# Sums applied at the copy of the slot inputs, a product moved out of the middle of another, and expert weights doubled at pairs 3, 5, 7 and 9

## The chip, the cores and the metric

The kernel runs on one core of one Trainium2 chip. The metric is the device time of one execution in microseconds (us). The kernel before takes 405.17 us, the median of three runs (404.94 to 406.31). Everything is float32; products of TensorE read float32 or, in the last stage, pairs of rounded values (high part and rest).

## What is computed

Three layers in a row: causal attention in a window of 128 positions, a soft mixture of experts (8 experts with 4 slots each), and a feed-forward layer with a squared ReLU.

```python
scores = where((rel >= 0) & (rel < 128), q @ k.T / sqrt(64) - slope_h * abs(rel), -1e9)
attn = softmax(scores) @ v                    # 4 batches, 8 heads, 576 positions, 64
x = attn.transpose(0, 2, 1, 3).reshape(2304, 512)

logits = x @ phi                              # 2304 x 32
d = exp(logits - logits.max(0)); d /= d.sum(0) + 1e-9     # softmax over the tokens
slot_input = (d.T @ x).reshape(8, 4, 512)
slot_out[e] = relu(slot_input[e] @ w1[e]) @ w2[e]         # w1 512 x 1024, w2 1024 x 512
c = softmax(logits, axis=1)
y = c @ slot_out

out = relu(y @ w_in) ** 2 @ w_out             # 512 x 2048, 2048 x 512
```

## The kernel before

**Attention.** The work goes in 16 pairs of heads, u = 0 to 15 (4 batches with 4 pairs each), and in 72 steps of two chunks of 64 queries. One loop over the steps (L413) writes out the order of every engine's queue: the scores of the next step (emit_S), transposes, the products with v of a pair (emit_PV), then maxima, exponentials and sums. Work that belongs to a finished pair, such as the logits, is hung on a later step by the tables `side` and `side0` (L375 to L404) and issued by `run_side`.

**Loads.** All of them go through SP's queue. When a pair's last scores are issued, the loop loads query and key tiles of the pair after next (`load_q`, two tiles of 144 KiB and one of 288 KiB) and then one or two weight tiles of 1 MiB for later stages (`load_next_w`, L429). These fill a ring of 19 tiles; its 19 loads in attention are three of w1, seven more of w1 and nine of w2. At the end of attention, as buffers of attention come free, the rest of w1 follows: `load_extra` for six tiles or half tiles (w1 of the steps 3, 4, 5, 4, 6 and 7: 1, 0.5, 1, 0.5, 1 and 1 MiB), and `yw` (L493), which holds the weights of step 8. After that `pump` loads two pairs of f tiles (w_in and w_out) and the rest of w2 as ring tiles come free.

**The softmax over tokens.** It is kept as a running one: `nm` is the negative maximum so far for each row (4 groups of tokens by 32 slots), `zs` the sum, and `acc` the weighted sum of x, 128 rows by 512. For the last batch (b = 3) the steps stand written out after the loop, lines 466 to 539:

- logits of the remainder of pair 14 (L468), transposes of x (`emit_xn`), logits of pair 15, their copies into lgT and lgR, the new maximum, and `bm` (L479), the maxima spread over four columns by group;
- transposes of pair 15's x (X, L484; Y, L486), GpSimd's memset of siT (L494), transposes of all logits (W, L497), and the product `rep` by `bm` (G, L499) that gives each row the maxima of all four groups;
- the exponential dT (L501), `gm[0]` (L505), the factor between a group's maximum and that of all; the transposes of dT (L508, L509) and their copies into dn (L510, L511);
- R (L522, L524), dn by x in two halves of 256 columns, each added to acc (L529). Between the halves stands another product of `rep` (G, L528) that adds up the scaled sums of the four groups; from it come `gm[4]`, the reciprocal, and `ef` (L533), a matrix of 128 by 32 that adds up the groups, scaled with both factors;
- X (L537), acc by ef, four blocks of 128 rows, and the copy into siT (L539), where `diag` puts every slot into the columns of its own expert. All else in siT is zero.

**Experts.** `w1_step` (L608) takes siT by the w1 tile of a step into H, 16 steps with four products each; after the first eight the result is transposed and put through the ReLU (`emit_hT`), and 16 steps take it by w2 into O (L729). Then the combination weights, w_in and the slots' outputs are multiplied, and the last layer runs in units of 768 tokens by 128 features (emit_h, L768; emit_g, L811).

`keep_warm` issues products of the identity with itself whose result nobody reads.

Of the kernel before, what the change touches and what calls it, by code (L numbers as in the profile page):

```python
# [11 lines left out]
AF = mybir.ActivationFunctionType  # L12
# [16 lines left out]
def attn_moe_relu2_kernel(ctx: ExitStack, tc: tile.TileContext, z0, q, k, v, phi, w1, w2, w_in, w_out, bias, cst, out):  # L29
# [250 lines left out]
    def emit_logr(u):  # L280
        b, kk = divmod(u, NPAIR)
        for g in (b,) if b % 2 else (b, b + 1):
            pe.matmul(out=L_t[b][32 * g:32 * g + 32, 128:192], lhsT=phi_sb[:, kk, :], rhs=xT[u][:, rem(b)],
                      start=False, stop=(kk == 3), tile_position=(0, 32 * g), skip_group_check=True)
# [92 lines left out]
    for u in range(NU):  # L377
        t0 = (NCH * u + 8) // 2 + LT
        add = lambda dt, f, *a: side.setdefault(t0 + dt, []).append((f, a))
        side0.setdefault(t0 + 1, []).append((u,))  # L380
        add(1, emit_xT, u)
        late = u == NU - 1
        if late:
            break
        if u < NU - 2:
            add(4, emit_xn, u)
        if u % NPAIR == NPAIR - 1:
            for x in range(u - 3, u + 1):
                add(3, emit_logits, x)
            for x in range(u - 3, u + 1):  # L390
                add(3, emit_logr, x)
        if u == NU - 2:
            for x in range(u - 2, u + 1):
                add(3, emit_logits, x)
            for x in range(u - 2, u):
                add(3, emit_logr, x)
        if u % NPAIR == NPAIR - 1:
            b = u // NPAIR
            add(4, emit_d0, b)
            add(5, emit_d1, b)  # L400
            add(6, emit_de, b)
            add(8, emit_d2, b)
            add(9, emit_d3, b)
            add(9, emit_d4, b)  # L404
# [8 lines left out]
    for t in range(NS + LT + 1):  # L413
# [3 lines left out]
        if t + 1 < NS:  # L417
            emit_S(t + 1)
            if t in (0, 2):
                keep_warm("B", 1, idle)  # L420
            for u, c, n, e in info[2 * t + 2:2 * t + 4]:
                if c == NCH - 1:
                    if u + NQ < NU:
                        load_q(u + NQ)
                    if u == 0:
                        load_v(1)
                        sp.dma_start(out=tbl[:, 384:], in_=bias[:, 384:])
                        sp.dma_start(out=phi_sb, in_=phi)
                    for _ in range(0 if u == 0 else 2 if u > NU - 4 or u == 5 else 1):  # L429
                        load_next_w()  # L430
        if 0 < t - LT < NS:
            emit_T(t - LT)
# [32 lines left out]

    u, b = NU - 1, NB - 1
    p = slice(32 * b, 32 * b + 32)
    emit_logr(u - 1)  # L468
    emit_xn(u - 1)
    emit_logits(u)  # L470
    emit_logr(u)
# [19 lines left out]
    yw = six.tile([128, 4, 512], F32, name="yw")  # L491
    wt[wkey("w1", 8)] = yw
    sp.dma_start(out=yw, in_=w1[wkey("w1", 8)[1]].rearrange("p (a b) -> p a b", a=4))  # L493
    pool.memset(siT, 0.0)  # L494
    W = bank("B", "W")
    for bb in range(4):
        pe.transpose(W[:, 128 * bb:128 * bb + 128], lg(bb), ident)  # L497
    G = bank("S", "G")
    pe.matmul(out=G[:, 0:4], lhsT=rep, rhs=bm, start=True, stop=True)  # L499
    act.activation(out=xn_all[:, :, sl], in_=X.rearrange("p (g d) -> p g d", g=4), func=AF.Copy)  # L500
    act.activation(out=dT, in_=lg(b, 256), func=AF.Exp, bias=nm, scale=1.0, accum_out=stat[:, 4:5])  # L501
    act.activation(out=stat[:, 5:6], in_=stat[:, 3:4], func=AF.Exp, bias=nm, scale=-1.0)
    act.activation(out=xnr[:, sl], in_=Y[:, 0:128], func=AF.Copy)
    dve.tensor_reduce(out=gm[:, 1:2], in_=G[:, 0:4], axis=AX.X, op=ALU.min)
    act.activation(out=gm[:, 0:1], in_=nm, func=AF.Exp, bias=gm[:, 1:2], scale=-1.0)  # L505
    dve.scalar_tensor_tensor(out=zs, in0=zs, scalar=stat[:, 5:6], in1=stat[:, 4:5], op0=ALU.mult, op1=ALU.add)
    X = bank("T", "X")
    pe.transpose(X[:, 0:128], dT[:, 0:128], ident)  # L508
    pe.transpose(X[:, 128:256], dT[:, 128:256], ident)  # L509
    dve.tensor_copy(out=dn[:, 0:128], in_=X[:, 0:128])  # L510
    dve.tensor_copy(out=dn[:, 128:160], in_=X[:, 128 + 32 * b:160 + 32 * b])  # L511
    dve.tensor_tensor(out=gm[:, 2:3], in0=gm[:, 0:1], in1=zs, op=ALU.mult)
    act.activation(out=lgT.rearrange("p (h x) -> p h x", h=2)[:, :, 0:256], in_=W.rearrange("p (h x) -> p h x", h=2), func=AF.Copy)
    W = bank("xa", "W")
    pe.transpose(W[0:64, 0:128], lgR, ident)
    act.activation(out=lgNR, in_=W[0:64, 0:128], func=AF.Copy)
    keep_warm("S", 1)
    for hf in range(2):
        cl = slice(256 * hf, 256 * hf + 256)
        R = bank("T", "R")  # L520
        for g in range(4):
# [1 line left out]
                      tile_position=(0, 32 * g), skip_group_check=True)  # L523
        pe.matmul(out=R[p, 0:256], lhsT=dn[:, 128:160], rhs=xnr[:, cl], start=False, stop=True,  # L524
                  tile_position=(0, 32 * b), skip_group_check=True)
        if hf == 0:
            G = bank("S", "G")
            pe.matmul(out=G[:, 0:1], lhsT=rep, rhs=gm[:, 2:3], start=True, stop=True)  # L528
        dve.scalar_tensor_tensor(out=acc[:, cl], in0=acc[:, cl], scalar=stat[:, 5:6], in1=R[:, 0:256], op0=ALU.mult, op1=ALU.add)  # L529
        if hf == 0:  # L530
            dve.tensor_scalar(out=gm[:, 3:4], in0=G[:, 0:1], scalar1=1e-9, scalar2=None, op0=ALU.add)
            dve.reciprocal(out=gm[:, 4:5], in_=gm[:, 3:4])
            dve.tensor_scalar(out=ef, in0=e32, scalar1=gm[:, 0:1], scalar2=gm[:, 4:5], op0=ALU.mult, op1=ALU.mult)  # L533
    keep_warm("S", 1)
    X = bank("S", "X")
    for kk in range(4):
        pe.matmul(out=X[:, 32 * kk:32 * kk + 32], lhsT=acc[:, 128 * kk:128 * kk + 128], rhs=ef, start=True, stop=True)  # L537
    keep_warm("S", 2)
    dve.tensor_copy(out=diag(siT, 4), in_=X[:, 0:128].rearrange("p (a e s) -> p a e s", a=4, e=E))  # L539
    ps1.close()  # L540
    psum[0] = ctx.enter_context(tc.tile_pool(name="ps2", bufs=2, space=bass.MemoryType.PSUM))
    NBUF.update({"S": 2, "xa": 2, "T": 1, "U": 1, "xb": 1})
# [456 lines left out]
```

## Time and profile before

| | us |
|---|---|
| median of three runs | 405.17 (404.94 to 406.31) |
| the profiled execution | 405.26 |
| its span, first to last instruction | 403.3 |
| TensorE busy | 393.5 |
| VectorE busy | 291.7 |
| ScalarE busy | 245.3 |
| GpSimd busy | 90.4 |

Times in the profile count from the start of the span. Attention ends at about 130 us, the expert products start at 138.95 us and the last layer's products at about 175 us. An instruction's time in brackets is the idle time of its engine before it, with what ended it; "issue" means that the profile shows nothing it waited for. PE is TensorE's product, PEld its weight load, DVE VectorE, ACT ScalarE, POOL GpSimd, SP the engine that only issues DMAs. A float32 product takes two loads and two products; a transpose takes one of each.

### The profile page before, as it was taken

Reading aid. Unit: us, or ns where it says so; the run is one execution under the profiler, and the core shown is the slowest. Engines: PE = TensorE matmul, PEld = TensorE weight load, DVE = VectorE, ACT = ScalarE, POOL = GpSimd, SP = SyncE. Lnnn points to the kernel's source line nnn. Section 1 sums busy time; section 2 is a strip of 40 time slices with the busy share of each in tenths; the row PEclk is TensorE's granted clock in tenths of the full one; section 3 lists DMA queues with packets and bytes.
Section 4 is the critical chain, followed back from the end, with each engine's and each line's share of the span. In section 5 each row is a group of like instructions: output and inputs, shape, how many; then the busy total and the mean of one; then the engine's idle time right before and its main releaser. Section 6 shows DMA issues by size and latency. Waiting matters only on the chain.

```text
span 403.3 us, 7748 instructions
## 1 busy us (share of the span) xinstructions
PE 393.5 (98%) x2555; PEld 305.4 (76%) x2555; DVE 291.7 (72%) x957; ACT 245.3 (61%) x735; POOL 90.4 (22%) x188
## 2 busy tenths in 40 slices
PE   8999999999999999999999999999999999999995
PEld 7888878878876533378777888788877888888884
DVE  6798887879887685477778777697766874567455
ACT  5788878868876412177677765767657634443440
POOL 4545435334433041231211111112010000000000
PEclk9999999999999999999999999999999999999999
DMA  7879899768899999999305200000000040003004
GB/s 202 246 261 269 282 333 253 239 206 289 228 411 418 405 421 421 411 410 406 125 2 206 107 2 0 2 0 1 2 1 0 2 156 0 2 27 130 2 1 156
DMA packets 35944, 70.92 MB, mean 176 GB/s; under 512 B 20032, under 2 KB 21440, under 8 KB 31936
## 3 DMA queue, kind: packets, MB, share of 16 engines
q1 hardware_dynamic: 35328, 69.87, 48.1%
q10 hardware_dynamic: 576, 0.56, 0.4%
q8 instruction: 20, 0.33, 0.4%
q14 instruction: 20, 0.16, 0.1%
HBM read 65.70 MB, written 4.72 MB: 175 GB/s over the span
## 4 chain that ended last, share of the span: by engine, by line
PE 89%; DVE 6%; DMA 2%; ACT 1%; issue 1%; SPq 0%; POOL 0%; DVEq 0%; POOLq 0%; ACTq 0%
PE acc L811 49%; PE s L164 9%; PE xa L249 6%; PE h L768 4%; PE H L611 4%; PE O L729 3%; PE tp L215 2%; DVE ptb L239 2%; DMA kt<-in_k_dram 2%; PE X L290 1%; DVE p L172 1%; PE tq L217 1%; PE MX L697 1%; PE L L277 1%; DVE psum L829 1%; PE tq L223 1%
## 5 line engine op out<-in xcount | busy, mean ns | idle before, releaser
L811 PE MATMUL acc<-whl,arena_gh 128*128 128x512 f32 x864 | 218.2, 395 | 0.0
L811 PEld LDWEIGHTS acc<-whl,arena_gh 128*128 128x128 f32 x864 | 160.2, 188 | 37.1 <-issue 4.2
L797 DVE TENSOR_TENSOR arena_gh<-hT,arena_gh 128x384 fp32r<-128x384 f32 (+1 forms) x97 | 54.7, 564 | 33.3 <-ACT arena_gh L793 25.1
L196 POOL TENSOR_SCALAR p<-p,st 128x192 f32<-128x192 f32 (+1 forms) x142 | 56.2, 408 | 67.5 <-DVE ptb L239 28.1
L183 ACT ACTIVATE p<-p,st 128x192 f32<-128x192 f32 (+1 forms) x144 | 61.4, 429 | 11.6 <-DVE st L172 11.3
L780 ACT ACTIVATE acc<-h 128x384 f32<-128x384 f32 (+2 forms) x49 | 23.7, 484 | 67.3 <-PE h L768 67.2
L164 PE MATMUL s<-kt,zq 128*128 128x192 f32 (+2 forms) x288 | 58.3, 327 | 1.3 <-DMA kt<-in_k_dram 1.2
L657 POOL TENSOR_SCALAR yw<-f 128x512 f32<-128x512 f32 x32 | 26.0, 815 | 112.3 <-DVE arena_cin L674 59.8
L164 PEld LDWEIGHTS s<-kt,zq 128*128 128x128 f32 x288 | 44.8, 196 | 3.3 <-DVE ptb L239 0.9
L239 DVE COPY ptb<-tq 64x128 f32<-64x128 f32 x128 | 35.3, 281 | 14.8 <-PE tq L217 13.5
L172 DVE CUSTOM_DVE_ANT_0 p<-s,tbl 128x192 f32<-128x192 f32 (+1 forms) x144 | 41.7, 325 | 3.5 <-PE s L164 3.0
L237 ACT ACTIVATE ptb<-tp 128x256 f32<-128x256 f32 (+1 forms) x72 | 25.0, 348 | 13.1 <-PE tp L215 11.0
L768 PE MATMUL h<-cst_sb,Mst 128*128 128x384 f32 x96 | 31.9, 337 | 0.3 <-DVE Mst L708 0.3
L249 PE MATMUL xa<-ptb,vt 128*64 128x256 f32 (+1 forms) x256 | 27.8, 359 | 0.0
L183 ACT ACTIVATION_READ_ACCUMULATOR p<-p,st 128x1 f32 x144 | 27.3, 189 | 0.0
L789 DVE TENSOR_TENSOR hT<-acc 128x384 f32<-128x384 f32 (+1 forms) x18 | 9.7, 541 | 23.6 <-ACT acc L780 23.6
L215 PE MATMUL tp<-cs,p 128*128 128x128 f32 x128 | 26.5, 275 | 0.2 <-DVE st L187 0.2
L793 ACT ACTIVATE arena_gh<-acc 128x384 fp32r<-128x384 f32 (+2 forms) x49 | 25.0, 509 | 0.7
L793 ACT ACTIVATE arena_gh<-hT 128x384 fp32r<-128x384 f32 x48 | 24.8, 516 | 0.6
L249 PEld LDWEIGHTS xa<-ptb,vt 128*64 128x64 f32 x256 | 17.0, 136 | 9.4 <-issue 1.9
L672 DVE SCALAR_TENSOR_TENSOR yw<-f,yw 128x512 int32<-128x512 int32 x32 | 22.5, 707 | 1.0
L780 ACT ACTIVATE hT<-h 128x384 f32<-128x384 f32 x48 | 22.7, 472 | 0.0
(176 smaller groups left out, 455.4 us busy)
## 6 DMA issues: line engine op xcount, KB each, us to landing
w_w<-in_w_dram SPq DMA_DIRECT2D x30, 1024.0 KB, 8.2
f<-in_w_in_dram SPq DMA_DIRECT2D x16, 512.0 KB, 10.2
f<-in_w_out_dram SPq DMA_DIRECT2D x16, 512.0 KB, 10.2
vt<-in_v_dram SPq DMA_DIRECT2D x16, 320.0 KB, 7.3
zq<-in_q_dram SPq DMA_DIRECT2D x30, 144.0 KB, 4.3
kt<-in_k_dram SPq DMA_DIRECT2D x15, 288.0 KB, 4.4
out_dram<-psum SPq DMA_DIRECT2D x11, 256.0 KB, 2.1
w_w<-in_w_dram SPq DMA_DIRECT2D x2, 512.0 KB, 10.0
```

What stands on the lines that cost most here:

```text
L164: pe.matmul(out=sb_t[t][:, 256 * i:256 * i + n], lhsT=zq[u % NQ][:, c].rearrange("p a b -> p (a b)"), rhs=kt_t[u][:, 64 * c + 64 - n:64 * ...
L172: dve.tensor_tensor_reduce(out=p, in0=sb_t[t][:, 256 * i:256 * i + n], in1=tbl[:, 192 * pr + 192 - n:192 * pr + 192], scale=-0.125, scalar ...
L183: act.activation(out=p, in_=p, func=AF.Exp, bias=st[:, i:i + 1], scale=-1.0, accum_out=st[:, 2 + i:3 + i])
L196: eng.tensor_scalar(out=p, in0=p, scalar1=st[:, 4 + i:5 + i], scalar2=0.0, op0=ALU.mult, op1=ALU.add)
L215: pe.transpose(A[:, i, :], P[:, e:e + 128], ident)
L239: dve.tensor_copy(out=dst, in_=src)
L249: pe.matmul(out=out, lhsT=v_t[u][:, j, po:po + 64], rhs=pt[:, a:b, po:po + 64], start=(j == 0 or (j == 3 and a == 2)), stop=(j == 4 or (j ...
L768: pe.matmul(out=hb[-1][:, 0:HB], lhsT=Mst[:, 128 * f:128 * f + 128], rhs=cst_sb[:, c0:c0 + HB], start=True, stop=True)
L780: act.activation(out=rbuf[hf][:, cl], in_=hb[hf][:, cl], func=AF.Relu)
L793: act.activation(out=lo_t[i][1][hf][:, 0, cl], in_=rbuf[hf][:, cl], func=AF.Square)
L797: eng.tensor_tensor(out=gh[hf][:, 1, cl], in0=g[hf][:, cl], in1=gh[hf][:, 0, cl].bitcast(F32), op=ALU.subtract)
L811: pe.matmul(out=acc_t[s], lhsT=gh[:, x, c0:c0 + 128], rhs=w[:, f % 2, y, :], start=(f in firsts and a == 0), stop=(f in lasts and a == 2))
```

## The change

The scaling with the sums moves from `ef` to the copy into siT: `ef` is now e32 by gm[0] alone, `ez` is ef by zs, one product of a matrix of ones with ez (after both halves of R) gives the sum for each of the 32 slots in every row, and its reciprocal `zr` multiplies X on its way into siT. The product G of L528 between the halves is gone, and so are the two calls of keep_warm before R and after it. The first G (rep by bm) and what follows from it come after the transposes of dT and their copies. GpSimd fills `ones` (in phi_sb's place) at the point where it zeroed siT, and zeroes siT after dn is copied; a copy of one column of dn on GpSimd stands ahead of that. The logits of pair 14's remainder move from behind the loop into the table `side`. In the loop, two weight tiles are loaded at the pairs 3, 5, 7 and 9 instead of 5, 13, 14 and 15; the total stays 19.

```diff
--- before.py
+++ after.py
@@ -392,7 +392,7 @@
         if u == NU - 2:
             for x in range(u - 2, u + 1):
                 add(3, emit_logits, x)
-            for x in range(u - 2, u):
+            for x in range(u - 2, u + 1):
                 add(3, emit_logr, x)
         if u % NPAIR == NPAIR - 1:
             b = u // NPAIR
@@ -426,7 +426,7 @@
                         load_v(1)
                         sp.dma_start(out=tbl[:, 384:], in_=bias[:, 384:])
                         sp.dma_start(out=phi_sb, in_=phi)
-                    for _ in range(0 if u == 0 else 2 if u > NU - 4 or u == 5 else 1):
+                    for _ in range(0 if u == 0 else 2 if u in (3, 5, 7, 9) else 1):
                         load_next_w()
         if 0 < t - LT < NS:
             emit_T(t - LT)
@@ -465,7 +465,6 @@
 
     u, b = NU - 1, NB - 1
     p = slice(32 * b, 32 * b + 32)
-    emit_logr(u - 1)
     emit_xn(u - 1)
     emit_logits(u)
     emit_logr(u)
@@ -491,30 +490,34 @@
     yw = six.tile([128, 4, 512], F32, name="yw")
     wt[wkey("w1", 8)] = yw
     sp.dma_start(out=yw, in_=w1[wkey("w1", 8)[1]].rearrange("p (a b) -> p a b", a=4))
-    pool.memset(siT, 0.0)
+    ones = phi_sb.rearrange("p a b -> p (a b)")
+    pool.memset(ones, 1.0)
     W = bank("B", "W")
     for bb in range(4):
         pe.transpose(W[:, 128 * bb:128 * bb + 128], lg(bb), ident)
-    G = bank("S", "G")
-    pe.matmul(out=G[:, 0:4], lhsT=rep, rhs=bm, start=True, stop=True)
     act.activation(out=xn_all[:, :, sl], in_=X.rearrange("p (g d) -> p g d", g=4), func=AF.Copy)
     act.activation(out=dT, in_=lg(b, 256), func=AF.Exp, bias=nm, scale=1.0, accum_out=stat[:, 4:5])
     act.activation(out=stat[:, 5:6], in_=stat[:, 3:4], func=AF.Exp, bias=nm, scale=-1.0)
     act.activation(out=xnr[:, sl], in_=Y[:, 0:128], func=AF.Copy)
-    dve.tensor_reduce(out=gm[:, 1:2], in_=G[:, 0:4], axis=AX.X, op=ALU.min)
-    act.activation(out=gm[:, 0:1], in_=nm, func=AF.Exp, bias=gm[:, 1:2], scale=-1.0)
     dve.scalar_tensor_tensor(out=zs, in0=zs, scalar=stat[:, 5:6], in1=stat[:, 4:5], op0=ALU.mult, op1=ALU.add)
     X = bank("T", "X")
     pe.transpose(X[:, 0:128], dT[:, 0:128], ident)
     pe.transpose(X[:, 128:256], dT[:, 128:256], ident)
     dve.tensor_copy(out=dn[:, 0:128], in_=X[:, 0:128])
     dve.tensor_copy(out=dn[:, 128:160], in_=X[:, 128 + 32 * b:160 + 32 * b])
-    dve.tensor_tensor(out=gm[:, 2:3], in0=gm[:, 0:1], in1=zs, op=ALU.mult)
+    pool.tensor_copy(out=stat[:, 15:16], in_=dn[:, 159:160])
+    pool.memset(siT, 0.0)
+    G = bank("S", "G")
+    pe.matmul(out=G[:, 0:4], lhsT=rep, rhs=bm, start=True, stop=True)
     act.activation(out=lgT.rearrange("p (h x) -> p h x", h=2)[:, :, 0:256], in_=W.rearrange("p (h x) -> p h x", h=2), func=AF.Copy)
+    dve.tensor_reduce(out=gm[:, 1:2], in_=G[:, 0:4], axis=AX.X, op=ALU.min)
+    act.activation(out=gm[:, 0:1], in_=nm, func=AF.Exp, bias=gm[:, 1:2], scale=-1.0)
     W = bank("xa", "W")
     pe.transpose(W[0:64, 0:128], lgR, ident)
     act.activation(out=lgNR, in_=W[0:64, 0:128], func=AF.Copy)
-    keep_warm("S", 1)
+    ez, zr = dT[:, 128:160], dT[:, 160:192]
+    dve.tensor_scalar(out=ef, in0=e32, scalar1=gm[:, 0:1], scalar2=None, op0=ALU.mult)
+    dve.tensor_scalar(out=ez, in0=ef, scalar1=zs, scalar2=None, op0=ALU.mult)
     for hf in range(2):
         cl = slice(256 * hf, 256 * hf + 256)
         R = bank("T", "R")
@@ -523,20 +526,17 @@
                       tile_position=(0, 32 * g), skip_group_check=True)
         pe.matmul(out=R[p, 0:256], lhsT=dn[:, 128:160], rhs=xnr[:, cl], start=False, stop=True,
                   tile_position=(0, 32 * b), skip_group_check=True)
-        if hf == 0:
-            G = bank("S", "G")
-            pe.matmul(out=G[:, 0:1], lhsT=rep, rhs=gm[:, 2:3], start=True, stop=True)
         dve.scalar_tensor_tensor(out=acc[:, cl], in0=acc[:, cl], scalar=stat[:, 5:6], in1=R[:, 0:256], op0=ALU.mult, op1=ALU.add)
-        if hf == 0:
-            dve.tensor_scalar(out=gm[:, 3:4], in0=G[:, 0:1], scalar1=1e-9, scalar2=None, op0=ALU.add)
-            dve.reciprocal(out=gm[:, 4:5], in_=gm[:, 3:4])
-            dve.tensor_scalar(out=ef, in0=e32, scalar1=gm[:, 0:1], scalar2=gm[:, 4:5], op0=ALU.mult, op1=ALU.mult)
-    keep_warm("S", 1)
+    G = bank("S", "G")
+    pe.matmul(out=G[:, 0:32], lhsT=ones, rhs=ez, start=True, stop=True)
+    dve.tensor_scalar(out=zr, in0=G[:, 0:32], scalar1=1e-9, scalar2=None, op0=ALU.add)
+    dve.reciprocal(out=zr, in_=zr)
     X = bank("S", "X")
     for kk in range(4):
         pe.matmul(out=X[:, 32 * kk:32 * kk + 32], lhsT=acc[:, 128 * kk:128 * kk + 128], rhs=ef, start=True, stop=True)
     keep_warm("S", 2)
-    dve.tensor_copy(out=diag(siT, 4), in_=X[:, 0:128].rearrange("p (a e s) -> p a e s", a=4, e=E))
+    dve.tensor_tensor(out=diag(siT, 4), in0=X[:, 0:128].rearrange("p (a e s) -> p a e s", a=4, e=E),
+                      in1=zr.rearrange("p (e s) -> p e s", e=E).unsqueeze(1).to_broadcast([128, 4, E, SPE]), op=ALU.mult)
     ps1.close()
     psum[0] = ctx.enter_context(tc.tile_pool(name="ps2", bufs=2, space=bass.MemoryType.PSUM))
     NBUF.update({"S": 2, "xa": 2, "T": 1, "U": 1, "xb": 1})
```

## Rows read from the trace of the kernel before

**Rows 1.** The page: busy time by engine; shares of the chain that ended last
```profile
PE 393.5 (98%) x2555; PEld 305.4 (76%) x2555; DVE 291.7 (72%) x957; ACT 245.3 (61%) x735; POOL 90.4 (22%) x188
PE 89%; DVE 6%; DMA 2%; ACT 1%; issue 1%; SPq 0%; POOL 0%; DVEq 0%; POOLq 0%; ACTq 0%
```

**Rows 2.** Waits, 118 to 176 us: who waited, total us, times, longest
```profile
PEld H L611 <- issue: 7.4, 27, 0.3
```

**Rows 3.** Timeline of the hand-off: start, duration, engine, line, operation, idle before
```profile
...
134.74 0.16 PEld L522 LDWEIGHTS R<-xn_all,dn 128*32 128x32 f32 x8 [0.24 <-DVE dn L510]
...
135.74 0.30 PEld L528 LDWEIGHTS G<-stat,cs 128*128 128x128 f32 x2 [0.41 <-issue]
...
136.05 0.16 PEld L522 LDWEIGHTS R<-xn_all,dn 128*32 128x32 f32 x8
...
137.05 0.30 PEld L98 LDWEIGHTS warm<-cs 128*128 128x128 f32 x2 [0.41 <-issue]
...
137.16 0.48 DVE L529 SCALAR_TENSOR_TENSOR acc<-acc,stat,R 128x256 f32<-128x256 f32 x1 [0.23 <-PE R L524]
137.27 0.97 PEld L537 LDWEIGHTS X<-ef,acc 128*128 128x128 f32 x8
...
138.46 0.29 DVE L539 COPY siT<-X 128x128 f32<-128x128 f32 x1 [0.82 <-PE X L537]
...
138.95 0.19 PEld L611 LDWEIGHTS H<-w_w,siT 128*32 128x32 f32 x8 [0.27 <-issue]
...
138.98 0.29 DVE L559 TENSOR_TENSOR xnr<-lgT,acc 128x128 f32<-128x128 f32 x1
```

**Rows 4.** Timeline around the last pair: the remainder's logits and what follows
```profile
...
127.64 0.33 PEld L283 LDWEIGHTS L<-xT,phi_sb 128*32 128x32 f32 x4
...
130.44 0.14 PEld L283 LDWEIGHTS L<-xT,phi_sb 128*32 128x32 f32 x2
...
130.67 0.42 PEld L290 LDWEIGHTS X<-cs,xT 128*128 128x128 f32 x4
```

**Rows 5.** Timeline: GpSimd's memset of siT beside VectorE, and VectorE alone
```profile
...
132.66 0.95 POOL L494 MEMSET siT<- 128x1024 f32 x1 [5.69 <-PE Y L486]
...
133.12 0.51 DVE L479 TENSOR_SCALAR bm<-cs,stat 128x4 f32<-128x4 f32 x1
...
134.60 0.18 DVE L511 COPY dn<-X 128x32 f32<-128x32 f32 x1
```

**Rows 6.** Windows of 8 us: busy time by engine, granted clock, DMA share, GB/s
```profile
...
36.00:44.00 8.00, 8.00 (x108) 7.22 (x105) 6.78 (x37) 5.68 (x26) 3.75 (x10) 1.00 0.78 265
44.00:52.00 8.00, 7.73 (x65) 5.70 (x65) 6.87 (x41) 6.91 (x30) 3.96 (x10) 1.00 0.87 295
...
84.00:92.00 8.00, 8.00 (x70) 7.04 (x70) 6.35 (x34) 5.49 (x23) 2.76 (x8) 1.00 0.63 196
...
132.00:140.00 8.00, 7.41 (x64) 4.77 (x67) 4.89 (x21) 3.45 (x13) 0.95 (x1) 1.00 1.01 410
```

**Rows 7.** Key tile of the ninth pair: issue, landing time, first weight load
```profile
...
53.63 0.61 SPq L135 DMA_DIRECT2D kt<-in_k_dram  x1
...
DMA to landing us min/median/max: 5.2/5.2/5.2
...
59.42 0.53 PEld L164 LDWEIGHTS s<-kt,zq 128*128 128x128 f32 x4
```

**Rows 8.** Last expert weights: issues, landing time of yw, weight loads that waited
```profile
...
128.77 3.15 SPq L83 DMA_DIRECT2D w_w<-in_w_dram  x4
...
132.63 0.33 SPq L493 DMA_DIRECT2D yw<-in_w_dram  x1
...
DMA to landing us min/median/max: 13.3/13.3/13.3
...
145.98 0.16 PEld L611 LDWEIGHTS H<-yw,siT 128*32 128x32 f32 x8 [0.84 <-DMA yw<-in_w_dram]
...
168.47 0.31 PEld L729 LDWEIGHTS O<-w_w,hT 128*32 128x32 f32 x8 [0.55 <-DMA w_w<-in_w_dram]
```

## The prediction

> **What bounds the kernel now.** I read the page first: TensorE is busy for 98% of the span, and the chain that ended last lies on it for 89% [rows 1]. So only time in which TensorE waits, or an instruction that leaves its queue, can change the total. The waits of the stretch after attention come next. In the first product's weight loads 27 gaps of 0.27 us are put down to issue [rows 2]; they are the rhythm of four row groups, not a wait. Two loads stand out: the one on yw with 0.84 us and one in the second product with 0.55 us, both behind a DMA [rows 8]. Less their ordinary 0.27 to 0.30 us these are 0.56 and 0.25 us of real waiting. The timeline of the hand-off shows the rest: from 134.74 to 138.95 us one chain runs through R in two halves, acc, X, the copy into siT and the first expert load [rows 3]. The windows, last, say that the DMA engines are full there (share 1.01, 410 GB/s) and that TensorE's granted clock is 1.00, its upper level, 2.4 GHz [rows 6].
>
> **The change, part by part.** Times are in the profiled execution: 405.26 us, of which 403.3 us are span and 1.96 us lie around it. It is 0.09 us above the median of the runs, 405.17 us.
>
> *The sum of the exponentials leaves the middle of R.* Now the product G of line 528 stands between the two halves of R. From its load to that of the second half it takes 136.05 - 135.74 = 0.31 us [rows 3], and the second half, acc (L529), X and siT follow one on another. Taken out: -0.31 us. The new G (ones against ez) stands after the second half, where one keep-warm call stood. That call took 137.27 - 137.05 = 0.22 us up to X's first load [rows 3]; the new one has the same two loads as L528, so at most 0.31 us. X's later half waits for acc anyway, so between 0 and 0.09 us comes back; I take 0.09. The first, earlier G (rep against bm) moves from before the transposes of dT to behind them, into the gap of 0.24 us in which TensorE waits for dn [rows 3], where another keep-warm call is removed. The transposes may start up to 0.1 us sooner; they wait for the exponential too, so I take 0.
>
> *ScalarE and VectorE.* The exponential of gm now comes after the copy of lgT. Its readers are ef and ez, needed by the new G and by X, 2 us later. VectorE loses one small product; add and reciprocal grow from one column to 32, and ez is new. A copy of 128x32 out of PSUM takes 0.18 us [rows 5], so each is below some 0.2 us. Add and reciprocal run behind the second acc while TensorE works on X, which is ready 0.82 us after acc at the latest [rows 3]: two times 0.2 fit. If that cover were gone, they would cost up to 0.4 us. The copy into siT becomes a product of the same size; the copy took 0.29 us and a 128x128 product with a broadcast operand 0.29 us [rows 3]: 0.
>
> *GpSimd.* The memset of siT moves behind dn's copy, held there by a one-column copy. It takes 0.95 us [rows 5] and siT isn't written until 138.1 us, so GpSimd itself is in time. But VectorE's L479, four columns, took 0.51 us and ended at 133.63, 0.02 us after the memset, while a copy of 32 columns takes 0.18 us without one [rows 5]. The memset now lies where ef and ez are made. It can start when L511 ends, at 134.78, and a little later for the copy ahead of it; it ends at 135.8 to 136.1. If ef is held to its end, ef, ez and the first acc (0.48 us) follow, the last done at about 137.0, and the second acc, due at 137.16 - 0.31 = 136.85, starts up to 0.15 us late. Bounds 0 to 0.3 us; I take 0 in the sum and give the hold a case below. The Trainium skill, SBUF — State Buffer, section "SBUF: two separate sides", says that VectorE and GpSimd share one port pair under an exclusive lock and that the loser blocks for the other's whole instruction. The row of L479 agrees. By that rule ef is surely held, and the sum would be up to 0.15 us less of a gain, 404.2 to 404.35; without it the sum stands. The new memset of ones (128 columns of those 1024) needs the last reader of phi and has 4 us until its use: 0.
>
> *The remainder's logits of pair 14* leave the place after the last pair's products, where their two loads hold TensorE for 130.67 - 130.44 = 0.23 us, and join four like them that take 0.33 us, 0.08 us each [rows 4]. Two more there cost 0.16 us on the same queue, ahead of the last transposes and the last pair's products. Difference -0.07 us, with bounds 0 and -0.2; I take -0.05.
>
> *Weights.* Pairs 3, 7 and 9 load two tiles instead of 13, 14 and 15; pair 5 loads two before and after. Three tiles of 1 MiB leave the end of SP's queue; at 410 GB/s [rows 6] each takes 2.56 us. From 128.77 us on SP issues 1 + 0.5 + 1 + 1 MiB and then yw [rows 8]: 4.5 MiB or 11.5 us, which from an empty queue would be over at 140.3. yw landed at 132.63 + 13.3 = 145.9, so up to 5.6 us of older loads lay ahead. Three tiles fewer are 7.7 us fewer: the queue is empty at 128.77, and with 2 or 3 us of start (0 isn't seen in any row; the key tile with two tiles ahead took 5.2 [rows 7]) yw lands at about 142 to 143. It is wanted at 145.98 - 0.56 = 145.4, or 145.1 with the shorter hand-off. The wait is gone: -0.56 us. Behind yw lie two f tiles and seven of w2, 9 MiB or 23 us: 145.9 + 23 = 168.9, about where the load at 168.47 waited [rows 8]; then 165 to 166, wanted at 167.3. Gone too: -0.25 us.
>
> What is late next? Not a DMA; TensorE's own queue through both products. The f loads come 3 us sooner as well, but the stage after them waits on ScalarE: 0, with up to -0.4 in the range.
>
> *The price of the earlier tiles.* Each delays the query and key tiles of the pair after next. DMA idles for 0.22 x 8 + 0.13 x 8 = 2.8 us between 36 and 52 us, and for 0.37 x 8 = 3 us between 84 and 92 [rows 6]: room for 2.56. The narrowest cover I found is pair 8's key tile: landed 53.63 + 5.2 = 58.8, first used from 59.42, so 0.6 us [rows 7]. Price 0, bound +2.2 us (the third rival).
>
> **Sum.** -0.31 + 0.09 - 0.05 - 0.56 - 0.25 = -1.08 us, so 405.26 - 1.08 = 404.2 us.
>
> **Rivals.** First, the hold by the memset swallows what the hand-off gains: 405.26 - 0.56 - 0.25 - 0.05 + 0.1 = 404.5. For it: L479; against: ef isn't wanted before X, at 137.27 now [rows 3], and the later acc, not the first, sets the pace. Second, the tiles don't come sooner, since SP's queue is filled from elsewhere. Then yw lands at 145.9 as now, and whatever the hand-off gains is waited for again: 405.2. Against: in the code only the first two extra tiles, 1.5 MiB, are issued between the ring's last tile and 128.77. Third, slower: the tile of pair 3 is not taken up by the idle time. The key tile of pair 8 then lands at 58.8 + 2.56 = 61.4 instead of 59.42, TensorE stands for 1.9 us, and pair 9's for some 0.3 more: 404.2 + 2.2 = 406.4, beyond it if pair 7's does the same. It decides from 0.6 us of delay on; the 2.8 us idle speak against. Fourth, more gain: the earlier f loads also clear VectorE and GpSimd around the start of the last stage, and dT's transposes start sooner: 403.6. Fifth, the two removed keep-warm calls let the clock fall to 1.2 GHz. No stretch shows that level, through waits of 0.24 us and more, but if the 4.2 us from 134.74 to 138.95 ran at half the clock, it would be up to 4 us: 405.5 to 408.
>
> **How the numbers follow.** Forecast 404.2 (403.7 to 404.6): 0.57. Memset 404.5: 0.12. No sooner 405.2: 0.07. Late keys 406.4 and over: 0.09. More gain 403.6: 0.11. Clock: 0.04. What a measurement can tell here is about 0.3%, 1.2 us: faster is below 403.95, slower above 406.4. The fourth rival and the lower part of the forecast give 0.34 for faster; late keys and half of the clock 0.11 for slower; the rest is 0.55. The range leaves out most of the third and fifth rivals and the lowest edge: 403.4 to 405.4.
>
> **What would show it.** In the changed profile R's halves should follow each other with loads 1.0 us apart, the first expert load start some 0.3 us sooner after the last pair's products, and yw and the second product have no load behind a DMA. VectorE's ef beside the memset shows the first rival, a wait on the key tile around 43 to 60 us the third, a granted clock below 1.00 the fifth. The forecast is wrong if the first load of the last stage's products is less than 0.8 us sooner.

## The result, and the profile after

The changed kernel takes 407.81 us (median of 18 runs, 404.93 to 411.31) against 405.27 us for the kernel before, measured beside it (18 runs, 404.66 to 407.79): ratio 1.0053 [1.0034, 1.0072]. The ratio leaves out the longest of after's runs, which counts as a slow one; the medians of all runs lie 2.54 us apart. The loss is small but clear of the noise, and the time lies outside the range that was given. The profiled execution of after took 406.08 us, one of the quicker ones; its span is 404.0 us, 0.7 more than before's 403.3. So its trace shows the pattern of the loss, not the whole of it. Four of the 18 runs, at 409.2 to 410.4 us, had a mean granted clock of 0.995 to 0.996; none of these was profiled.

The page of after, busy time by engine and the chain that ended last by engine:

```profile
PE 392.7 (97%) x2551; PEld 304.2 (75%) x2551; DVE 292.4 (72%) x957; ACT 245.7 (61%) x735; POOL 90.6 (22%) x190
...
PE 85%; DMA 5%; DVE 5%; ACT 2%; issue 1%; SPq 1%; POOL 0%; DVEq 0%; POOLq 0%; ACTq 0%
```

Against [rows 1] the chain has moved from TensorE (89% to 85%) to DMA (2% to 5%). The waits of the attention stage, 8 to 126 us, say which DMA (who waited; total us, times, longest):

```profile
PE s L164 <- DMA kt<-in_k_dram: 2.2, 3, 0.9
...
PEld s L164 <- DMA kt<-in_k_dram: 0.8, 1, 0.8
```

The products wait 2.2 us on key tiles in three places (the load row is one of these waits once more, seen from the loads). Before had 1.2 us in the same stretch, all of it before 16 us, on the first keys:

```profile
PE s L164 <- DMA kt<-in_k_dram: 1.2, 2, 0.7
```

Which ones they are in after, TensorE's products say (start, duration, engine, line, operation, idle before and its releaser):

```profile
9.88 1.01 PE L164 MATMUL s<-kt,zq 128*128 128x64 f32 x6 [0.93 <-DMA kt<-in_k_dram]
...
44.02 0.68 PE L164 MATMUL s<-kt,zq 128*128 128x64 f32 x4 [0.69 <-DMA kt<-in_k_dram]
...
60.63 0.71 PE L164 MATMUL s<-kt,zq 128*128 128x64 f32 x4 [0.61 <-DMA kt<-in_k_dram]
```

The first belongs to the start; the others are the keys of pairs 6 and 8. The time from one pair's first product of L249 to the next shows what each cost: set beside before's, after is 0.45 us ahead up to pair 3 (35.27 against 35.72), 0.33 behind from 44.97 on, 1.19 from 61.59 on and 1.48 from 78.18 on. So late keys cost 0.78 + 0.86 + 0.29 = 1.93 us here. (The last 0.29 us is put down to the keys of pair 10, which landed at 77.1 us with their first product at 77.24; the profile names no wait there.)

The span falls into three parts at two such products, the second pair's (22.18 us in before, 21.73 in after) and the last pair's (128.54 and 130.14), here before's two and then after's:

```profile
22.18 1.74 PE L249 MATMUL xa<-ptb,vt 128*64 128x256 f32 x16
...
128.54 1.73 PE L249 MATMUL xa<-ptb,vt 128*64 128x256 f32 x16
...
21.73 1.73 PE L249 MATMUL xa<-ptb,vt 128*64 128x256 f32 x16
...
130.14 1.73 PE L249 MATMUL xa<-ptb,vt 128*64 128x256 f32 x16
```

| | start to second pair | to last pair | to the end | span |
|---|---|---|---|---|
| before | 22.18 | 106.36 | 274.76 | 403.3 |
| after | 21.73 | 108.41 | 273.86 | 404.0 |
| difference | -0.45 | +2.05 | -0.90 | +0.7 |

The first part is the start, which varies from one execution to the next and has nothing of the change in it. The stage that was to become shorter did, and the stage that pays for it lost more: the +2.05 are the 1.93 us of late keys and 0.11 of two loads that the change moves ahead of the last pair.

The windows of after, columns as in [rows 6] (the last two are DMA share and GB/s):

```profile
36.00:44.00 8.00, 7.33 (x100) 6.47 (x97) 6.75 (x39) 5.92 (x26) 3.30 (x9) 1.00 1.09 305
44.00:52.00 8.00, 7.71 (x65) 5.83 (x66) 6.17 (x38) 6.59 (x28) 3.74 (x10) 1.00 1.07 309
52.00:60.00 8.00, 7.67 (x66) 6.48 (x64) 6.42 (x34) 6.07 (x25) 3.37 (x9) 1.00 1.07 293
60.00:68.00 8.00, 7.36 (x63) 6.26 (x62) 6.13 (x40) 6.29 (x26) 3.31 (x9) 1.00 1.07 314
68.00:76.00 8.00, 7.73 (x95) 6.50 (x94) 5.91 (x34) 5.18 (x24) 3.81 (x10) 1.00 1.09 297
76.00:84.00 8.00, 7.75 (x64) 6.16 (x65) 6.60 (x40) 7.35 (x33) 3.14 (x8) 1.00 1.00 299
84.00:92.00 8.00, 8.00 (x67) 5.95 (x63) 6.03 (x32) 5.00 (x20) 2.74 (x7) 1.00 0.85 283
```

The share went from 0.78 and 0.87 [rows 6] to 1.09 and 1.07, but the rate only from 265 and 295 to 305 and 309 GB/s. Full of weight tiles alone the same engines move 410 [rows 6]. In the mix of attention they are full at about 300. (The share adds up the times of packets and can pass 1.)

Pair 8's key tile, the one the prediction named as the narrowest, in after: its issue at 54.0 us, and the time from issue to landing.

```profile
L135 SPq DMA_DIRECT2D kt<-in_k_dram x1: 613/613/613, 54.0 to 54.0; - x1
...
DMA to landing us min/median/max: 6.6/6.6/6.6
```

6.6 us instead of 5.2, so it lands at 60.6, where its first load began at 59.42 in before [rows 7]; this is the wait at 60.63 above. The two key tiles before it and the two behind it took 6.4 to 8.2 us (in before 3.9 to 5.6).

The hand-off in after, timeline:

```profile
129.13 0.44 PEld L283 LDWEIGHTS L<-xT,phi_sb 128*32 128x32 f32 x6
...
130.14 1.49 PEld L249 LDWEIGHTS xa<-ptb,vt 128*64 128x64 f32 x16 [0.17 <-issue]
...
132.04 0.42 PEld L290 LDWEIGHTS X<-cs,xT 128*128 128x128 f32 x4
...
136.03 0.37 PEld L525 LDWEIGHTS R<-xn_all,dn 128*32 128x32 f32 x11 [0.32 <-DVE dn L506]
...
136.25 0.95 POOL L509 MEMSET siT<- 128x1024 f32 x1
...
136.50 0.74 DVE L519 TENSOR_SCALAR ef<-cs,stat 128x32 f32<-128x32 f32 x1 [0.36 <-ACT stat L514]
...
137.28 0.24 DVE L520 TENSOR_SCALAR dT<-ef,stat 128x32 f32<-128x32 f32 x1
...
138.11 0.97 PEld L536 LDWEIGHTS X<-ef,acc 128*128 128x128 f32 x8
...
139.29 0.29 DVE L538 TENSOR_TENSOR siT<-X,dT 128x128 f32<-128x128 f32 x1 [0.32 <-PE X L536]
...
139.80 0.19 PEld L611 LDWEIGHTS H<-w_w,siT 128*32 128x32 f32 x8 [0.27 <-issue]
```

And the two loads that waited in [rows 8]:

```profile
146.26 0.16 PEld L611 LDWEIGHTS H<-yw,siT 128*32 128x32 f32 x4 [0.27 <-issue]
...
169.23 0.26 PEld L729 LDWEIGHTS O<-w_w,hT 128*32 128x32 f32 x8 [0.60 <-DMA w_w<-in_w_dram]
```

From the last pair's first product to the first expert load it is 9.66 us instead of 10.41. yw no longer keeps a load waiting; the tile of the second product still does. The windows of this stretch, columns as above, show the granted clock at 1.00 throughout:

```profile
128.00:136.00 8.00, 7.11 (x88) 5.23 (x87) 4.21 (x17) 4.39 (x14) 0.65 (x2) 1.00 0.76 256
136.00:144.00 8.00, 7.86 (x74) 4.09 (x78) 6.74 (x28) 1.38 (x5) 1.07 (x2) 1.00 1.01 413
```

### The profile page after: what moved, and what is told of

Its sections match the earlier page's. It is cut to its first block, busy times and chain, and to the rows that moved or that the text cites. A ratio compares the mean times of both kernels' runs of the same rounds, so it can differ in the third digit from the quotient of the medians.

```text
span 404.0 us, 7740 instructions
## 1 busy us (share of the span) xinstructions
PE 392.7 (97%) x2551; PEld 304.2 (75%) x2551; DVE 292.4 (72%) x957; ACT 245.7 (61%) x735; POOL 90.6 (22%) x190
## 4 chain that ended last, share of the span: by engine, by line
PE 85%; DMA 5%; DVE 5%; ACT 2%; issue 1%; SPq 1%; POOL 0%; DVEq 0%; POOLq 0%; ACTq 0%
PE acc L811 49%; PE s L164 7%; PE xa L249 5%; DMA kt<-in_k_dram 5%; PE h L768 4%; PE H L611 4%; PE O L729 3%; PE tp L215 2%; DVE ptb L239 2%; DVE p L172 1%; PE X L290 1%; PE MX L697 1%; PE tq L217 1%; DVE psum L829 1%; PE MY L703 1%
## 5 line engine op out<-in xcount | busy, mean ns | idle before, releaser
L164 PEld LDWEIGHTS s<-kt,zq 128*128 128x128 f32 x288 | 43.9, 193 | 5.6 <-issue 2.7
L249 PE MATMUL xa<-ptb,vt 128*64 128x256 f32 (+1 forms) x256 | 27.8, 359 | 0.0
L249 PEld LDWEIGHTS xa<-ptb,vt 128*64 128x64 f32 x256 | 17.0, 136 | 9.5 <-issue 2.0
```

The source lines that it names most:

```text
L164: pe.matmul(out=sb_t[t][:, 256 * i:256 * i + n], lhsT=zq[u % NQ][:, c].rearrange("p a b -> p (a b)"), rhs=kt_t[u][:, 64 * c + 64 - n:64 * ...
L249: pe.matmul(out=out, lhsT=v_t[u][:, j, po:po + 64], rhs=pt[:, a:b, po:po + 64], start=(j == 0 or (j == 3 and a == 2)), stop=(j == 4 or (j ...
```

## Experiments

The theory (A): the weight tiles at pairs 3, 7 and 9 fill the DMA queue of the attention stage, key tiles land late, and TensorE stands; the new hand-off is sound. The rival: the hand-off itself costs the time (the memset's hold, the clock without the keep-warm calls), and the late keys of one profile are chance. Every kernel was timed beside the kernel before, whose median was 405.73 us beside the first four kernels below, 405.4 beside the next four and 405.56 beside the last four. Each kernel has one profiled execution, and what is read from it can differ in another.

**The new hand-off alone**, with the old places for the doubled tiles:

```diff
-                    for _ in range(0 if u == 0 else 2 if u in (3, 5, 7, 9) else 1):
+                    for _ in range(0 if u == 0 else 2 if u > NU - 4 or u == 5 else 1):
```

> The changed hand-off with the weight loads of before (two tiles at pairs 5, 13, 14 and 15). Theory A (the time is lost in attention, where the earlier weight tiles make query and key tiles late): the hand-off is some 0.6 us shorter, but yw lands where it did, near 145.9 us, so the wait for it grows from 0.56 to about 1.2 us and the time stays at 405.2, within 0.4. Theory B (the new order of the hand-off itself costs, by GpSimd's memset beside VectorE): 407 to 408.

Measured: 405.26 us, ratio 0.9993 [0.9976, 1.0009]. The loss is gone, as theory A had it, so the hand-off isn't its cause. No gain can be measured either. Its profiled execution (407.63 us, its longest) shows one reason, the products' side of the first expert product:

```profile
148.08 1.07 PE L611 MATMUL H<-yw,siT 128*32 128x512 f32 x8 [1.45 <-DMA yw<-in_w_dram]
```

With the old schedule yw comes late for the shorter hand-off (in this execution it also landed some 0.9 us later after the last pair's first product than in before), and TensorE stands for it: from the last pair to the end it takes 275.71 us there, 0.95 more than before, though the hand-off in it is 0.75 shorter. From the second pair to the last it is 106.48 us, after's loss of 2 us gone.

**The new places alone**, in the kernel before (the places-only kernel from here on):

```diff
-                    for _ in range(0 if u == 0 else 2 if u > NU - 4 or u == 5 else 1):
+                    for _ in range(0 if u == 0 else 2 if u in (3, 5, 7, 9) else 1):
```

> The kernel before with two weight tiles at pairs 3, 5, 7 and 9, hand-off untouched. Theory A: key tiles of pairs 6, 8 and 10 land after they are wanted, 2 to 3 us of TensorE waiting in attention, less the 0.56 us of yw: 407 to 408.5. Theory B: nothing lost in attention, 404.5 to 405.

Measured: 407.88 us, ratio 1.0053 [1.0028, 1.0077], the whole of the loss. Its profiled execution was its longest (411.01 us), and shows what long runs of after may look like. Waits, 8 to 126 us:

```profile
PE s L164 <- DMA kt<-in_k_dram: 5.1, 5, 2.2
...
PEld s L164 <- DMA kt<-in_k_dram: 1.2, 1, 1.2
```

The load row again repeats one of the products'. The longest, 2.2 us, lies at 17.64 us, ahead of the first double; it is the start's, which put this execution 2.59 us behind before's. From the second pair to the last it takes 109.44 us, 3.08 more than before (1.18, 1.19 and 0.71 at pairs 6, 8 and 10), and from there to the end 274.99 (before 274.76). The granted clock stays at 1.00 in all windows from 36 to 92 us: these 3 us are waiting and not a lower clock. The loss that theory A expected is there.

**The same total at other pairs**: doubles at 5, 8, 9 and 13, with the new hand-off. Against before, two doubles have moved, to 8 and 9, where after has three, at 3, 7 and 9. (The diff is the same line with another set; so it is below with one extra tile and with two.)

> The changed kernel with two weight tiles at pairs 5, 8, 9 and 13, the same total of 19. In the trace of before the DMA engines are nearly idle from 74 to 78 and from 83 to 87 us, right behind the loads of pairs 8 and 9. Theory A: these places take the tiles without delay to a key tile, the hand-off's 0.6 us and most of the wait on yw are gained: 404.0 to 404.4. Theory B, or if any tile that is loaded earlier costs: 407 and over.

Measured: 405.30 us, 0.9989 [0.997, 1.0007]. From the second pair to the last it takes 106.48 us. Key tiles land in 4.4 us at the median between 30 and 100 us, as before's in 4.5 (after's: 6.5). The two doubles at 8 and 9 cost nothing here; the gain of some 1 us that was expected isn't there either.

**A cheaper query tile**: after, with {3, 5, 7, 9} kept, but each pair's query tile loaded whole, its zero halves included, in one transfer of 128 rows instead of two of 64 rows. (Part of the edit: the filling of the tiles with zeros on GpSimd at the start goes too, and the host lays q out with its zeros.)

```diff
-        z = zq[u % NQ]
-        sp.dma_start(out=z[0:64, :, 0, :], in_=q[u, 0:64].rearrange("p (c t) -> p c t", t=64))
-        sp.dma_start(out=z[64:128, :, 1, :], in_=q[u, 64:128].rearrange("p (c t) -> p c t", t=64))
+        sp.dma_start(out=zq[u % NQ].rearrange("p c a b -> p (c a b)"), in_=q[u])
```

> The changed kernel, but each pair's query tile is loaded as one transfer of 128 rows of 4608 bytes, zeros among them, in place of two of 576 pieces of 256 bytes: twice the bytes, no small packets. Theory A1 (large packets take longer while other DMA engines still move small ones, so the slowest of the 16 engines falls behind): key tiles land some 2 us sooner and the time falls to 404 to 405. Theory A2 (only the bytes count): 0.3 MB more in each pair, key tiles later still, 409 and over.

Measured: 405.27 us, 0.9992 [0.9979, 1.0004]. Twice the bytes for the queries, and the loss is gone with the schedule untouched. Windows of this kernel:

```profile
36.00:44.00 8.00, 8.00 (x107) 6.99 (x106) 6.72 (x36) 5.72 (x27) 3.97 (x10) 1.00 1.01 408
...
60.00:68.00 8.00, 7.46 (x65) 6.40 (x65) 6.92 (x41) 6.55 (x28) 4.08 (x11) 1.00 1.00 377
```

With the engines full (share 1.01, in after 1.09) the queue now moves 408 instead of 305 GB/s, key tiles land in 5.2 us at the median, 6.4 at most, and from the second pair to the last it is 106.48 us again. The time is a little above A1's range, and A2 is out. So the mix was slow because of the query transfers, not because of its bytes.

**One extra tile at a time** beside pairs 5, 13 and 14 (pair 15's double given up): pair 3, pair 7, pair 9.

> The changed kernel with two weight tiles at pairs 3, 5, 13 and 14: of the three that the change moves only one, to pair 3. The same with the loads of before took 405.26 us. Theory A with pair 3 as the cause (its tile is still in the queue when the tiles of pairs 6 and 8 are wanted): 406.3 to 407.3, key tile of pair 6 landing over 6 us after its issue. Rival (no tile costs alone, only three together overfill the queue): 405.0 to 405.6.

> The changed kernel with two weight tiles at pairs 5, 7, 13 and 14: only one moved, to pair 7. Theory A: pair 10's key tile lands later by about one tile's 2.5 us, of which 3.5 us were spare, so 405.3 to 406.0, less than pair 3's. Rival (only three together): 405.0 to 405.6.

> The changed kernel with two weight tiles at pairs 5, 9, 13 and 14: only one moved, to pair 9, behind which the DMA engines are idle for 3 us. Theory A: 404.9 to 405.4, no key tile late. Rival (any tile moved to before pair 13 costs): 406 and over.

Measured: 405.64 us, 1.0013 [0.9987, 1.0039]; 405.05, 0.9996 [0.9976, 1.0017]; 405.31, 0.9996 [0.9977, 1.0016]. None costs anything that can be told in the median. From the second pair to the last the profiles give 107.32, 106.50 and 106.50 us: only the double at pair 3 shows, with 0.9 us. Most of it, 0.7 us, comes where the keys of pair 8 are late, behind the double at pair 5 that stays:

```profile
59.98 0.71 PE L164 MATMUL s<-kt,zq 128*128 128x64 f32 x4 [0.44 <-DMA kt<-in_k_dram]
```

So no double here was quite alone.

**Two halves, whole rows**: as the cheap query tile above, but in two transfers of 64 rows, each with its zeros, so that count and rows are those of after and the length of a row is that of the cheap one.

(Part of the edit, against after; the rest is that of the one transfer.)

```diff
+        z = zq[u % NQ].rearrange("p c a b -> p (c a b)")
+        sp.dma_start(out=z[0:64], in_=q[u, 0:64])
+        sp.dma_start(out=z[64:128], in_=q[u, 64:128])
```

> As the one with whole query tiles of 128 rows of 4608 bytes (405.27 us), but again two transfers for each pair, of 64 rows each, as the kernel before issues them. If the small packets were what made key tiles late: 405.0 to 405.8, as with one transfer. If it was the third transfer on SP's queue and the 0.6 us by which the key tile is issued later: 406.5 to 408.

Measured: 423.8 us, 1.0435 [1.0389, 1.0482]; neither expectation holds. The page's row of these transfers (count, KB each, median us from issue to landing):

```profile
zq<-in_q_dram SPq DMA_DIRECT2D x30, 288.0 KB, 7.9
```

The trace notes when each of the 16 DMA engines is through with a tile, and tiles land in the order of their issue. With the same bytes as in the one-transfer kernel, in the same long rows, the second half of pair 6's query tile, 288 KB, landed 1.20 us behind the first (43.33 and 44.53 us, the first engine to land each); in the one-transfer kernel the whole 576 KB landed 1.47 us behind the tile ahead (39.01 and 40.48). By these distances, which are an estimate since neighbours overlap, a transfer that covers 64 rows runs at about 245 GB/s against 400. After's 144 KB halves land 0.8 us apart (41.77, 42.58, 43.36, the last engine), 180 GB/s. These have pieces of 256 bytes as well as 64 rows; the kernel with whole rows shows that the 64 rows are enough for a loss, and what the short pieces add isn't separated.

The Trainium skill, SBUF — State Buffer, sections "Door 1: The DMA port swizzle (why `[64,N]` ≈ `[32,N]`)" and "Can I just issue two DMAs to hit both halves?", says this: 64 rows reach 8 of the 16 ports, and two such transfers don't run beside each other to make up for it. The two kernels agree, with 423.8 us against 405.27 us and a half of the bytes in 1.20 us against the whole in 1.47. The prediction hadn't drawn on it.

Here the waits also reached the clock. Waits, 8 to 126 us, and then three windows (columns as above; the seventh is the granted clock):

```profile
PE s L164 <- DMA kt<-in_k_dram: 13.8, 8, 3.2
...
PEld s L164 <- DMA kt<-in_k_dram: 2.4, 1, 2.4
```

```profile
47.00:50.50 3.50, 1.02 (x9) 0.89 (x11) 1.95 (x14) 1.21 (x7) 1.67 (x4) 0.99 1.03 331
50.50:53.90 3.40, 3.40 (x24) 2.30 (x24) 0.97 (x7) 1.74 (x8) 0.83 (x2) 0.50 1.01 185
53.90:57.00 3.10, 3.10 (x25) 2.91 (x22) 1.66 (x9) 2.37 (x11) 0.12 (x1) 1.00 1.06 247
```

TensorE was busy for 1.02 of 3.5 us, behind a key tile that was late, and then ran 3.4 us at the lower level, 1.2 GHz. The trace has four such stretches (from 50.5, 70.9, 91.4 and 118.7 us), each behind waits on key tiles.

**Two of the three**: doubles at 3, 5, 7 and 13.

> The changed kernel with two weight tiles at pairs 3, 5, 7 and 13. One of 3, 7 and 9 alone cost within 0.4 us of nothing, all three together 2.2 us. If doubles at every other pair add up in the queue (3, then 5, then 7): 406.5 to 407.5. If it takes all three: 405 to 405.8.

Measured: 406.71 us, 1.0035 [1.0019, 1.005]: about half of the loss. Waits of the attention stage and its fullest window, with the one behind it:

```profile
PE s L164 <- DMA kt<-in_k_dram: 2.3, 4, 1.1
```

Of these 2.3 us 0.9 belong to the start; the longest, 1.15 us at 77.20, is on the keys of pair 10, behind the doubles at 3, 5 and 7.

```profile
68.00:76.00 8.00, 7.96 (x95) 6.66 (x91) 5.90 (x35) 5.84 (x25) 3.16 (x8) 1.00 1.11 279
76.00:84.00 8.00, 6.69 (x59) 5.53 (x62) 5.65 (x37) 6.27 (x27) 3.16 (x8) 1.00 1.06 286
```

From the second pair to the last it is 107.90 us, 1.54 over before. By the medians one tile costs -0.4 to +0.2 us, 3 and 7 together +1.15, all three +2.15 (each against the kernel before beside it; the last is the places-only kernel). With as many doubles up to pair 9, at 5, 8 and 9, nothing was lost. So the cost isn't one price per tile: it depends on where the doubles stand, and grows where the queue has no slack between one double and the next.

**The hand-off with a later yw**: old places, but the tile that is loaded last (yw) is used at step 10 instead of 8 of the first expert product. (Part of the edit: the order of the ring's loads changes to match.)

```diff
-    wt[wkey("w1", 8)] = yw
+    wt[wkey("w1", 10)] = yw
-        elif not 3 <= i < 9:
+        elif not (3 <= i < 8 or i == 10):
```

> The changed hand-off, the weight loads of before (pairs 5, 13, 14, 15), and yw used two expert steps later: the tile of step 10 goes into yw and that of step 8 into the ring, so the wait on yw has 1.7 us more. If the new hand-off is 0.6 us shorter and only yw holds it back: 404.0 to 404.5. If the hand-off gains nothing: 404.7 to 405.0, by the old wait of 0.56 alone.

Measured: 405.95 us, 1.0005 [0.9981, 1.0028]; the expected gain wasn't there in the median. In the profile no load waits for yw, from the second pair to the last it takes 106.52 us (before 106.36, the two moved loads are 0.11 of the difference), and from there to the end 274.10, 0.66 less than before. That is 0.16% and lies inside the interval. And the start, up to the second pair, lies between 21.47 and 24.77 us in the profiles of this study, a spread of five times the gain.

**Everything that held**: doubles at 5, 8, 9 and 13 and the later yw, and the same with the one-transfer query tile.

> The changed hand-off, two weight tiles at pairs 5, 8, 9 and 13, and yw used at step 10. With those pairs and yw at step 8 the time was 405.3. Expected from removing the rest of the waits on yw: 404.6 to 405.1; no change from 405.3 if those waits were under 0.3 us.

> As the one before, with each pair's query tile loaded whole, as one transfer of 128 rows with zeros among them. If a transfer into 64 rows moves at half the rate and holds up what follows it on SP's queue, key tiles land sooner and with less spread: 404.0 to 404.7 and a narrow spread of the single runs. If the bytes count: 405.5 and over.

Measured: 405.31 us, 1.0003 [0.9981, 1.0026], and 405.64, 1.0001 [0.9987, 1.0016]. The first lost 2.0 us to late keys in its profiled execution (108.49 us from the second pair to the last, products waiting 2.1 us on key tiles there, 1.3 of it behind the doubles at 8 and 9), with places that lost nothing in the run above; so these too are near the edge. The one-transfer query tile keeps 106.52, and its single runs spread less, over 2.3 us instead of 4.5, as expected; the gain in the median that was expected with it didn't come. No version is measurably faster than the kernel before.

## Why the prediction was wrong

The forecast was -1.08 us, all of it behind the last pair, at a price of 0 for the earlier tiles. After's profile shows -0.90 behind the last pair and +1.93 for late keys. The price was not 0, and it is the step that failed: idle time in a mean share of the DMA engines was taken for room. The bound that the prediction gave for it, +2.2 us, took in what came (1.93 us in this trace, 2.15 by the medians of the new places alone), but the range left most of it out.

**The price of the earlier tiles** failed at two places. The first is the room: 2.8 us in 16 us were read from the mean share of the engines. A mean share below 1 isn't room for a transfer, since tiles land in the order of their issue and a tile has landed only when the slowest of its 16 engines is through. Between 36 and 78 us that is 0.9 to 2.2 us behind the first in before's key tiles, 2.4 to 3.7 in after's, and 0.5 to 2.0 with the one-transfer query tile and the same places. Between 36 and 76 us after's share rose to 1.07 to 1.09 and stayed there; so each double began before the one ahead had been worked off. The second is the size: a tile was taken at 410 GB/s, 2.56 us, from a stretch of nothing but weights [rows 6]. On the first engine that holds, but in attention it shares the queue with query halves that move at 180 GB/s: the second tiles of after's doubles at 3, 5 and 7 land 2.5 to 2.7 us behind the first tiles by the first engine and 3.1 to 3.4 by the last. Each place alone is within what a median can tell, two cost 1.15 us, three 2.15. The 0.6 us margin of pair 8's key tile [rows 7] was rightly named as the point that decides: it took 1.4 us longer to land, 0.9 of it between its first engine and its last (3.02 us instead of 2.10), TensorE's products waited 0.61, and the pairs behind it came 0.86 later.

So the third rival, late keys at 406.4 us and over, was the case, with its mechanism in the main as told (a tile ahead in the queue, not the slower engines) and a chance that was too low; the 2.8 us idle that spoke against it were the misread figure. It was priced on pair 8 and 9 alone; the queue stays full up to 84 us, and pairs 6 and 10 came late too.

**The middle of R.** Predicted -0.31 + 0.09 = -0.22 us; from R's first load to X's first it is 138.11 - 136.03 = 2.08 instead of 2.53 us, so -0.45. The halves' loads aren't 1.0 us apart but interleave from 136.49 on: without the product between them the second half starts while the first still runs. The right mechanism, under-sized by half.

**The remainder's logits.** Two loads more ahead of the last pair cost 0.44 - 0.33 = 0.11 us, and from the last pair's first product to L290's load it is 1.90 instead of 2.13, so -0.23: net -0.12, predicted -0.05 to -0.07. Another 0.08 came between L290 and R. In all the hand-off gained 0.75 us, the same 9.65 to 9.66 us in every kernel of this study that has it, whatever its schedule; that part is shown.

**The memset** held ef just as the first rival said: 0.74 us, ended at 137.24, 0.04 behind the memset, while ez of the same size took 0.24 and before's ef, with no memset beside it, 0.30. L479's product bm shows the same from the other side: 0.51 us beside the memset in before [rows 5], 0.23 in after, where none runs beside it. The hold cost nothing: the first acc, held back to 137.43, is done when R's last product ends at 137.96, and the second acc can't start before that.

**yw's wait** is gone, but not for the reason given and not for 0.56 us. yw landed at 134.00 + 11.5 = 145.5 us, not at 142 to 143. The queue had run empty, as predicted (share 0.09 from 129.3 to 131 us), but the stage came 1.6 us later, so that its loads were issued from 130.30 on, and from 131 to 136 us they moved 298 GB/s, not 410. What ended the wait is that yw landed 0.4 us sooner than in before while the first expert load came 0.85 later. So the sign of the second rival, yw at 145.9, nearly came, though not because the queue was filled from elsewhere. And the wait hadn't cost what the load row says. The products of before around it:

```profile
143.70 2.36 PE L611 MATMUL H<-w_w,siT 128*32 128x512 f32 x20
145.99 1.06 PE L611 MATMUL H<-yw,siT 128*32 128x512 f32 x8
```

TensorE's products show no idle time there, though the load is put down with 0.84 us. In after the load of yw at 146.26 has its product at 146.69: here loads run 0.43 us ahead of products, and a wait of a load eats this lead first (in before the load and its product start at 145.98 and 145.99). From the first expert load to the first product on yw it was 145.99 - 138.95 = 7.04 us in before and is 6.89 in after: the wait was worth 0.15 us. The Trainium skill, TensorE: Matmul & The Clock Gate, section "Part 2: What happens when you issue a matmul", says that the queue pulls weight loads ahead of products in flight; these rows agree, and it was the reason to look for the wait on the products' side.

**The second product's wait**, predicted to go (-0.25 us), stayed: 0.60 us in the load row. For the same reason it costs nothing. From the first expert load to the transposes behind that product after takes 170.33 - 139.80 = 30.53 us, and the places-only kernel, whose load there doesn't wait, 175.15 - 144.62 = 30.53.

So the sum behind the last pair came out nearly right (-0.90, or -0.79 with the two loads that went ahead of the last pair) by luck, by two errors that cancel: -0.75 from the hand-off in place of -0.27, and -0.15 from the waits in place of -0.81.

**The clock** didn't fall in the hand-off (1.00 from 128 to 144 us); the keep-warm calls weren't missed. It fell where key tiles were late in the kernel with two whole half-row transfers, another place than the fifth rival thought. In four runs of after its mean was 0.4 to 0.5% below 1; where it fell there isn't shown.

What stays open: how much of after's loss of 2.5 us in the median is waiting and how much clock, since none of after's long runs was profiled (the 3.08 us at a clock of 1.00 in the places-only kernel speak for the first); why the 64-row transfers leave some engines so far behind; and what the hand-off is worth by itself, since its 0.75 us show in each trace but in no median.

## What to carry to other kernels

Price a moved load at the rate of the stretch that it moves into, with that stretch's own transfers in the queue, and look for room in the margin between landing and first use of each transfer behind it, not in a mean share of the DMA engines. Test a schedule of several moved loads as a whole: here each alone cost nothing that a median could tell, and the three together, which made four doubles at every other pair, 0.5%. Where weight loads run ahead of products, as here, a wait in the loads is a loss only as far as the products show it too.

## What the runs showed of the hardware that was not expected

- Transfers of 64 rows, by their landings some 180 to 245 GB/s, slow the queue for all behind them: the full queue moved 305 GB/s with them and 408 with one transfer of 128 rows and twice the bytes. Splitting the same bytes into two half-row transfers made the kernel 4.35% slower than before.
- What came late was the slowest engine: between 36 and 78 us the last of the 16 was through with a key tile 2.4 to 3.7 us behind the first in after, and 0.5 to 2.0 us with whole query tiles in one transfer.
- Weight loads ran 0.43 us ahead of products in the first expert product, so that 0.84 us in front of a load cost 0.15 us.
- In the kernel with two whole half-row transfers the granted clock was 0.50 for 3.4 us four times in one execution, each time behind a wait on a key tile; the longest of these waits was 3.2 us.
